# Strassen's held PSUM banks as tiles of their own, and narrow score tiles for the first twelve attention units

## The chip, the cores and the metric

The kernel runs on one core of one Trainium2 chip. The metric is the device time of one execution in microseconds. Time before: a median of 747.47 us over three runs (745.8 to 748.61).

## The reference

Window attention with eight heads (four with a plain window of 32 keys, four with every fourth key of the last 128), then a feed-forward layer that takes the maximum of three products. Everything is fp32.

```python
# q, k, v: [8, 8, 576, 64]
rel = pos[:, None] - pos[None, :]
mask_plain = (rel >= 0) & (rel < 32)                       # heads 0 to 3
mask_dil = (rel >= 0) & (rel < 128) & (rel % 4 == 0)       # heads 4 to 7
scores = where(mask, q @ k.T / 8, -1e9)
attn = softmax(scores) @ v
x = attn.transpose(0, 2, 1, 3).reshape(4608, 512)
h = maximum(maximum(x @ w1, x @ w2), x @ w3)               # w1, w2, w3: [512, 768]
out = h @ w_out                                            # w_out: [768, 512]
```

## The kernel before

**Number format.** An fp32 product is made of three matmuls on a high and a low part of each operand: high by high, high by low, low by high. All large matmuls therefore come in threes.

**Attention.** The work is cut in 64 units: half a batch (288 tokens) times a pair of heads, NPAIR = 4 pairs to a half. A unit takes scores into a couple of PSUM banks (one bank per head of the pair), reduces the maximum, takes exponentials, sums, normalises, turns the weights around (keys to partitions) and multiplies by the values; the result goes, split in high and low parts, into x. The first LEAN = 12 units are made by `dense` (L588): blocks of 96 queries by 128 keys (72 by 104 in the dilated heads), masks added by a matmul with the identity (L622), scores (L629), three passes of VectorE over 768 or 832 columns (L646, L465, L662), transposes on TensorE through a second couple (L711), a copy back, values (L735); forms C and D normalise afterwards, with sums from TensorE (L745). A letter of FORMS per unit picks the variant. The other units are made by `attention` and `behind` (L841, L888): tiles of 32 queries by 64 keys, 96 rows of three query blocks at a time, half as many columns, masks at L861, scores at L875, maximum L908, exponentials L919 or L931, and six 32x32 transposes on VectorE (L970) into PT, whose unused places stay zero; values at L982. They come in visits of two units (`visited`, `products`), whose matmuls stand together in TensorE's order.

**Feed-forward, plain part.** The first 1152 tokens (four halves) go through `ffn` (L1032) in three tiles of 384 tokens: up projections at L1048 in the two banks of the tag "ffn", then down at L1101.

**Feed-forward, Strassen part.** The other 3456 tokens go in four passes of 864. In each, nine blocks of the up projections (six feature pairs are three double rows times the three weights) are made with seven products instead of eight: `combine` (L1216) forms the token sums, `multiplied` (L1312) the products, each six matmuls of 128x432 (L1348). Products accumulate across each other in PSUM. D (product 0) and A (product 1) go to the two "ffn" banks; bB and bC are held for a whole pass:

```python
held = [buf("b", f"held{i}") for i in range(2)]
```

The order on TensorE is, per block: 0 into D, 1 into A, 6 of the block before into bC, 2 into bB, 3 into A, 4 into bC, 5 into bB. Between them ScalarE copies bB<-bA after product 1 (`ab`, L1430) and bC<-bB after product 2 (`bc`, L1437), both by the line L458. VectorE (L465) takes the maximum or the sum out of the banks: the put of product 6 reads bC after product 6 and has to come before `bc` overwrites it. After each pass the down projection runs (L1491). The product weights come from DRAM, 256 KB each, on the queue of SP into six slots, reused in turn.

**PSUM.** Eight banks: three tiles `banks_0` to `banks_2` of two banks each (couples, tag "b", six slots), and two `bank_i` of one (tag "ffn"). A request of width 2 takes a couple, one of width 1 half of one. Waits are set by tile: an instruction that touches one half of a couple is ordered behind earlier work on either half by another engine. bB and bC are the halves of one couple. Matmuls whose output is named "banks" write into couples.

**Order.** Nothing is issued as it is described: each step is handed to a planner (`Plan`, L112) with its cost by engine, its dependencies and its buffers. `deadlines` works due times back from the feed-forward steps, with a slack per kind of step (UNIT_SLACK, COMBINE_SLACK and so on); the planner then picks, step by step, the engine and the step that can start soonest, the most urgent first, chooses slots (`couple`, `single`), and issues in that order. Where TensorE would stand idle for long in the early part it adds a filler matmul (L1595), which keeps the array busy and computes nothing. The costs are estimates in the code: they set the order, and the chip's semaphores do the rest.

Of the kernel before, what the change touches and what calls it, by code (L numbers as in the profile page):

```python
# [34 lines left out]
SLOTS = 6  # L35
TAKEN = 70
# [4 lines left out]
FORMS = "adDaaaAaCADA"  # L41
# [7 lines left out]
SPILL = 0.103  # L49
# [3 lines left out]
UNIT_PACE, UNIT_SLACK, UNIT_LEAD = 1.728, 2.588, 2.639  # L53
FILL = 0.22
BURSTS, BURST = (21, 35), 16
WEIGHT_PACE, WEIGHT_SLACK, WEIGHT_LEAD = 0.544, 0.749, 1.374
# [7 lines left out]
class Buf:  # L64


    def __init__(self, pool, tag, limit, shape, dtype, name):
        self.pool, self.tag, self.limit = pool, tag, limit
        self.shape, self.dtype, self.name = shape, dtype, name
        self.users = 0  # L70
        self.number = None
        self.end = 0.0
        self.slot = None
        self.t = None
        self.width = 1

# [35 lines left out]
class Plan:  # L112
# [54 lines left out]
    def room(self, st, slots):  # L167
# [6 lines left out]
        for tag in set(new):  # L174
            k = new.count(tag)
            left = slots[tag]
            for b in st.bufs:
                if b.tag == tag and b.slot is None and b.width == 2:
                    t, i = self.couple(left)
# [6 lines left out]
    def couple(self, free):  # L186

        when = {i: t for t, i in free}
        return min(((max(t, when[i + 1]), i) for i, t in when.items() if not i % 2 and i + 1 in when), default=(1e9, 0))

    def single(self, free, at):

        held = {i for _, i in free}
        return min(free, key=lambda x: (max(x[0], at), x[1] ^ 1 in held, x))
# [30 lines left out]
    def order(self, fill=None):  # L225
# [11 lines left out]
        order = []  # L237
        live, since = {"dve": None, "pool": None}, 0.0
        fills, must, bursts = 0, 0, list(BURSTS)
        while len(order) - fills < len(self.steps):  # L240
            best = None
            for e, cands in waiting.items():
                now = free[e]
                for st in cands:
# [3 lines left out]
                    if st.bufs:  # L248
                        at = max(at, self.room(st, slots))
# [34 lines left out]
            for b in sorted(st.bufs, key=lambda b: -b.width):  # L284
                if b.slot is None:
                    if b.width == 2:
                        b.slot = self.couple(slots[b.tag])[1]
                    else:
                        b.slot = self.single(slots[b.tag], at)[1]
                    slots[b.tag] = [x for x in slots[b.tag] if not 0 <= x[1] - b.slot < b.width]  # L290
                    self.given[b.tag] = self.given.get(b.tag, 0) + 1
            if e == "sp":
# [30 lines left out]
            for b in st.bufs:  # L323
                b.users -= 1
# [20 lines left out]
def tile_dilated_window_attention__then__maxout_ffn(  # L345
# [78 lines left out]
    KEPT["b"] = [x[:, i] for x in couples for i in range(2)] + couples  # L424
# [29 lines left out]
    nc.gpsimd.memset(strips[:, 0, :WIN], NEG)  # L454

# [132 lines left out]
    def dense(u):  # L588

        half, p = divmod(u, NPAIR)  # L590
        b, hf = divmod(half, 2)
        dil = int(p >= 2)
        nb, nq, wk = (4, 72, 104) if dil else (3, 96, 128)
        nw = nb * wk
        k_step = 104 if dil else 96
        form = FORMS[u]
        runs = [(0, 2)] if form.islower() else [(0, 1), (1, 2)]
        blockwise, late = form in "bdBD", form in "cdCD"
        kb, kload, v, vload = loads(u, (None, None))
        W, mx, sm = buf("W", f"W{u}"), buf("mx", f"mx{u}"), buf("sm", f"sm{u}")  # L600
        sp, tp = (buf("b", f"{x}{u}", width=2) for x in ("s", "pt"))

        def S4(j0, j1):
            return sp.t[:96, j0:j1, :nw].rearrange("p j (n k) -> p j n k", k=wk)

        def W4(j0, j1):
            return W.t[:nq, nw * j0 : nw * j1].rearrange("p (j n k) -> p j n k", j=j1 - j0, k=wk)

        def by_row(x, j0, j1):
            return x.t[:nq, j0 * nb : j1 * nb].rearrange("p (j n) -> p j n", j=j1 - j0)  # L610

        def spread(x, j0, j1):
            return by_row(x, j0, j1).unsqueeze(3).broadcast_to([nq, j1 - j0, nb, wk])

        def scores(_):

            for j in range(2):
                if dil or hf:
                    m = masks[:96, hf : hf + 1, :wk].broadcast_to([96, nb, wk])
                else:  # L620
                    m = masks[:96, :nb, :wk]
                nc.tensor.matmul(  # L622
                    S4(j, j + 1)[:, 0], identb[:96, :96], m, start=True, stop=False, skip_group_check=True
                )
            for i in range(nb):
                for j in range(2):
                    d = slice(64 * j, 64 * j + 64)
                    k0 = HALF + k_step * i
                    nc.tensor.matmul(  # L629
                        S4(j, j + 1)[:nq, 0, i],  # L630
                        kb.t[d, nq * i : nq * i + nq],
                        kb.t[d, k0 : k0 + wk],
                        start=False,
                        stop=True,
                        skip_group_check=True,
                    )

        s = plan.add(
            {"pe": 0.3 + 2 * nw * 0.000435 + nb * (wk / 600 + 0.01)}, scores, [kload], [kb, mx, W, sp], rows=96
        )  # L640
        expd, last = [], []
        for j0, j1 in runs:
            n = nw * (j1 - j0)

            def most(_, j0=j0, j1=j1):
                nc.vector.tensor_reduce(  # L646
                    by_row(mx, j0, j1), S4(j0, j1)[:nq], axis=mybir.AxisListType.X, op=ALU.max, negate=True
                )

            def eighth(e, j0=j0, j1=j1):  # L650
                a = mx.t[:nq, j0 * nb : j1 * nb]
                (nc.vector if e == "dve" else nc.gpsimd).tensor_scalar(a, a, 0.125, None, ALU.mult)

            def less(_, j0=j0, j1=j1):
                tt("dve", W4(j0, j1), S4(j0, j1)[:nq], spread(mx, j0, j1), ALU.add)

            def expo(_, j0=j0, j1=j1):
                a = W.t[:nq, nw * j0 : nw * j1]
                nc.scalar.activation(a, a, AF.Exp, scale=0.125)

            def total(_, j0=j0, j1=j1):
                nc.vector.tensor_reduce(by_row(sm, j0, j1), W4(j0, j1), axis=mybir.AxisListType.X, op=ALU.add)  # L662

            t = plan.add({"dve": dve(n)}, most, [s], [sp, mx])
            if blockwise:
                t = plan.add({"dve": 0.165, "pool": 0.22}, eighth, [t], [mx])
                for m in range(j0 * nb, j1 * nb):

                    def expo_b(_, m=m):
                        j, i = divmod(m, nb)  # L670
                        nc.scalar.activation(
                            W.t[:nq, wk * m : wk * m + wk],
                            S4(j, j + 1)[:nq, 0, i],
                            AF.Exp,
                            bias=mx.t[:nq, m : m + 1],
                            scale=0.125,
                            accum_out=sm.t[:nq, m : m + 1],
                        )

# [976 lines left out]
```

## Time and profile before

| | |
|---|---|
| median of three runs | 747.47 us |
| the profiled execution | 746.38 us |
| its span | 744.6 us |
| granted TensorE clock, mean | 0.997 |
| TensorE matmuls busy | 706.9 us, 95% |
| VectorE busy | 506.9 us, 68% |
| GpSimd busy | 294.6 us, 40% |
| ScalarE busy | 291.3 us, 39% |
| first matmul of the plain feed-forward | at 54.04 us |
| moved by DMA | 140.30 MB, 188 GB/s |

PE is the matmul side of TensorE, PEld its weight loads, DVE is VectorE, ACT ScalarE, POOL GpSimd, SP the queue that issues the DMAs. In a timeline a row is a run of like instructions: start, length, how many, and in brackets how long the engine had been idle and what ended that. The length of a run of matmuls reaches a little past the start of the next run, since matmuls overlap; differences of starts are exact. In the chain of waits each row is a stretch of the path that ends last. A row of the waits reads: who waited for whom, microseconds in total, times, longest.

### The profile page before, as it was taken

Reading aid. Unit: us, or ns where it says so; the run is one execution under the profiler, and the core shown is the slowest. Engines: PE = TensorE matmul, PEld = TensorE weight load, DVE = VectorE, ACT = ScalarE, POOL = GpSimd, SP = SyncE. Lnnn points to the kernel's source line nnn. Section 1 sums busy time; section 2 is a strip of 40 time slices with the busy share of each in tenths; the row PEclk is TensorE's granted clock in tenths of the full one; section 3 lists DMA queues with packets and bytes.
Section 4 is the critical chain, followed back from the end, with each engine's and each line's share of the span. In section 5 each row is a group of like instructions: output and inputs, shape, how many; then the busy total and the mean of one; then the engine's idle time right before and its main releaser. Section 6 shows DMA issues by size and latency. Waiting matters only on the chain.

```text
span 744.6 us, 16812 instructions
## 1 busy us (share of the span) xinstructions
PE 706.9 (95%) x6492; PEld 602.3 (81%) x6492; DVE 506.9 (68%) x943; ACT 291.3 (39%) x1015; POOL 294.6 (40%) x376
## 2 busy tenths in 40 slices
PE   8979999999999999999999999899999989999998
PEld 5549888998998987887888888688888868888876
DVE  6978899879778665678766567996756795223240
ACT  5566643433345524335443434253343423122211
POOL 3778866674128111167510205761020475001042
PEclk9999999999999999999999999999999999999999
DMA  9969936536623778672487777248776613666511
GB/s 322 327 205 357 328 122 211 175 113 219 198 63 100 228 217 258 210 219 100 141 240 222 238 221 215 71 138 239 218 238 194 183 54 98 200 194 198 169 44 53
DMA packets 83807, 140.30 MB, mean 188 GB/s; under 512 B 7952, under 2 KB 32272, under 8 KB 83728
## 3 DMA queue, kind: packets, MB, share of 16 engines
q1 hardware_dynamic: 83728, 139.23, 60.0%
q8 instruction: 51, 0.84, 0.5%
q14 instruction: 28, 0.23, 0.1%
HBM read 113.25 MB, written 25.95 MB: 187 GB/s over the span
## 4 chain that ended last, share of the span: by engine, by line
PE 76%; DVE 10%; POOL 5%; ACT 4%; issue 2%; DMA 2%; SPq 0%; POOLq 0%; DVEq 0%; ACTq 0%
PE banks L1348 25%; PE bank L1348 14%; PE bank L1491 11%; PE bank L1048 10%; PE bank L1101 4%; PE banks L982 4%; ACT banks L458 3%; PE banks L875 3%; PE bank L1595 2%; DVE PT L970 2%; DVE h L465 2%; DVE hx L465 2%; DMA wS<-tmps 1%; POOL wu L465 1%; DVE tmps L465 1%
## 5 line engine op out<-in xcount | busy, mean ns | idle before, releaser
L1348 PE MATMUL banks<-t,wm 128*128 128x432 f32 x864 | 195.8, 368 | 20.3 <-ACT banks L458 14.5
L1348 PEld LDWEIGHTS banks<-t,wm 128*128 128x128 f32 x864 | 156.7, 188 | 49.9 <-ACT banks L458 33.6
L1348 PE MATMUL bank<-t,wm 128*128 128x432 f32 x648 | 139.9, 360 | 0.0
L970 DVE STREAM_TRANSPOSE PT<-W 32x192 f32<-32x192 f32 (+1 forms) x312 | 125.1, 401 | 7.2 <-POOL W L465 1.6
L1348 PEld LDWEIGHTS bank<-t,wm 128*128 128x128 f32 x648 | 121.5, 188 | 6.3
L1491 PE MATMUL bank<-wdn,h 128*128 128x512 f32 (+1 forms) x504 | 119.6, 394 | 4.9 <-DVE h L465 3.0
L1048 PE MATMUL bank<-xa,wu 128*128 128x384 f32 x648 | 118.2, 338 | 0.5 <-ACT tmps L458 0.5
L1491 PEld LDWEIGHTS bank<-wdn,h 128*128 128x128 f32 (+1 forms) x504 | 91.9, 184 | 29.6 <-DVE h L465 4.2
L1048 PEld LDWEIGHTS bank<-xa,wu 128*128 128x128 f32 x648 | 111.7, 188 | 2.8 <-ACT tmps L458 1.1
L931 ACT ACTIVATE W<-banks,mx 96x64 f32<-96x64 f32 x286 | 85.0, 315 | 30.4 <-PE banks L1348 12.1
L912 POOL TENSOR_SCALAR mx<-mx 96x8 f32<-96x8 f32 (+1 forms) x35 | 8.6, 245 | 139.6 <-DVE mx L908 139.5
L931 ACT ACTIVATION_READ_ACCUMULATOR W<-banks,mx 96x1 f32 x286 | 59.2, 207 | 0.0
L458 ACT COPY tmps<-bank 128x432 f32<-128x432 f32 (+1 forms) x51 | 25.8, 507 | 83.5 <-PE bank L1348 73.8
L465 POOL TENSOR_TENSOR W<-W,sm 96x384 f32<-96x384 f32 (+4 forms) x39 | 40.1, 1031 | 37.0 <-DVE sm L957 33.5
L908 DVE TENSOR_REDUCE mx<-banks 96x6 f32<-96x384 f32 (+1 forms) x52 | 30.0, 614 | 33.2 <-PE banks L875 33.2
L465 DVE TENSOR_TENSOR tmps<-banks,tmps 128x432 f32<-128x432 f32 (+1 forms) x52 | 30.6, 591 | 29.5 <-PE banks L1348 29.3
L460 POOL TENSOR_SCALAR h<-hx 128x256 fp32r<-128x256 f32 (+1 forms) x24 | 9.8, 415 | 94.0 <-DVE hx L465 88.3
L465 POOL TENSOR_TENSOR h<-hx,h 128x256 fp32r<-128x256 f32 (+1 forms) x52 | 40.9, 808 | 14.4 <-PE bank L1491 10.9
L952 POOL TENSOR_TENSOR sm<-sm,small_c 96x8 f32<-96x8 f32 (+1 forms) x46 | 12.1, 264 | 83.4 <-ACT W L931 68.1
L458 ACT COPY o<-bank 128x512 f32<-128x512 f32 (+1 forms) x35 | 20.5, 584 | 51.6 <-PE bank L1491 34.2
L465 DVE TENSOR_TENSOR hx<-banks,hx 128x432 f32<-128x432 f32 x24 | 14.5, 606 | 37.6 <-PE banks L1348 37.6
L1101 PE MATMUL bank<-wdn,h 128*128 128x512 f32 x162 | 38.6, 395 | 0.0
(137 smaller groups left out, 943.2 us busy)
## 6 DMA issues: line engine op xcount, KB each, us to landing
wm<-wS SPq DMA_DIRECT2D x252, 256.0 KB
k<-in_qk_d_dram SPq DMA_DIRECT2D x32, 352.0 KB
k<-in_qk_p_dram SPq DMA_DIRECT2D x32, 304.0 KB
wS<-tmps SPq DMA_DIRECT2D x18, 512.0 KB
st<-in_w_up_dram SPq DMA_DIRECT2D x14, 512.0 KB
v<-in_v_d_dram SPq DMA_DIRECT2D x32, 208.0 KB
out_dram<-o SPq DMA_DIRECT2D x25, 256.0 KB
v<-in_v_p_dram SPq DMA_DIRECT2D x32, 192.0 KB
```

The source lines that it names most:

```text
L458: nc.scalar.copy(dst, src)
L465: (nc.vector if eng == "dve" else nc.gpsimd).tensor_tensor(dst, a, b, op=op)
L875: nc.tensor.matmul(sp.t[32 * r : 32 * r + rows, j, at + 64 * n : at + 64 * n + nk], kb.t[d, q0 : q0 + rows], kb.t[d, k0 : k0 + nk], start= ...
L908: nc.vector.tensor_reduce(by_row(mx), S4(), axis=mybir.AxisListType.X, op=ALU.max, negate=True)
L931: nc.scalar.activation(W3()[:, m], S4()[:, m // nb, m % nb], AF.Exp, bias=mx.t[:96, m : m + 1], scale=0.125, accum_out=sm.t[:96, m : m + 1],)
L970: nc.vector.transpose(PT.t[c : c + 32, : 2 * nb, 32 * i : 32 * i + 32], W3()[32 * i : 32 * i + 32, :, 32 * e : 32 * e + 32],)
L982: nc.tensor.matmul(pv.t[64 * j : 64 * j + 64, nq * i : nq * i + nq], v.t[:wk, j, i, :], PT.t[:wk, nb * j + i, :nq], start=True, stop=True,)
L1048: nc.tensor.matmul(bank.t[:, :n], wu[f].t[:, g, wz, c, :], xa[c].t[:, xz, t0 : t0 + n], start=(m == 0 and c == 0), stop=(m == 2 and c == 3),)
L1101: nc.tensor.matmul(bank.t, hv(hs[f], hz)[:, s0 : s0 + 128], wdn[f].t[:, wz], start=(f == 0 and m == 0), stop=(f == NF - 1 and m == 2),)
L1348: nc.tensor.matmul(bank.t[:, :HP], wv[:, wz, c], t_of(i, xz)[:, c], start=(start and m == 0 and c == 0), stop=(m == 2 and c == 1), skip_gr ...
L1491: nc.tensor.matmul(bank.t[:rows], hz.t[:, f, :rows], wdn[f].t[:, wz], start=(f == 0 and m == 0), stop=(f == NF - 1 and m == 2),)
L1595: nc.tensor.matmul(idle.t, identb, masks.rearrange("p n k -> p (n k)"), start=True, stop=True)
```

## The change

1. **The held banks.** PSUM is now two couples and two tiles `single_0` and `single_1` of one bank. bB gets `single_0` and bC `single_1` as a fixed home, so neither shares a tile. Small outputs such as a unit's values may use the singles before the Strassen part begins.
2. **The planner** knows of the tile that a couple shares: `shared` and `seen_by` delay a step until the other engines have finished their last work on either half, and `single` prefers a bank that is free of this.
3. **The first twelve units** are made by `attention` and `behind`, one unit to a visit, and `dense` is gone. FORMS has a new meaning: a lower-case letter turns the weights with six 32x32 transposes on VectorE (u4, u5, u7 to u11), an upper-case one with transposes on TensorE through a couple and four copies (u0 to u3, u6). Four memsets on GpSimd clear the PT buffers at the start.
4. **Numbers of the planner**: slacks, paces and costs, among them 0.05 instead of 0.25 us for a visit's fixed cost and 12.5 instead of 14.0 ns for a small score matmul.

```diff
+COUPLES = 2
-FORMS = "adDaaaAaCADA"
+FORMS = "AAAAaaAaabaa"
-TILE_NS = 14.0
+TILE_NS = 12.5
-COMBINE_SLACK, PREPARE_SLACK, LOAD_SLACK = 25.759, 134.466, 0.15
+COMBINE_SLACK, PREPARE_SLACK, LOAD_SLACK = 12.814, 72.124, 0.5
...
-UNIT_PACE, UNIT_SLACK, UNIT_LEAD = 1.728, 2.588, 2.639
+UNIT_PACE, UNIT_SLACK, UNIT_LEAD = 2.0, 1.802, 5.094
...
+        for b in st.bufs:
+            if b.slot is None and b.home is not None:
+                at = max(at, next((t for t, i in slots[b.tag] if i == b.home), 1e9))
...
+    def shared(self, i, e):
+
+        return max((t + self.AFTER[o] + TO_PE * (e == "pe") for o, t in self.seen[i].items() if o != e), default=0.0)
...
-    couples = [ps.tile([128, 2, 512], F32, name=f"banks_{i}", bufs=1) for i in range(3)]
+    couples = [ps.tile([128, 2, 512], F32, name=f"banks_{i}", bufs=1) for i in range(COUPLES)]
...
+    singles = [ps.tile([128, 512], F32, name=f"single_{i}", bufs=1) for i in range(6 - 2 * COUPLES)]
+    KEPT["b"] = [x[:, i] for x in couples for i in range(2)] + singles + couples
...
+    for t in KEPT["PT0"][::-1] + KEPT["PT1"]:
+        nc.gpsimd.memset(t, 0.0)
...
+    def early(u):
+
+        sp = buf("b", f"s{u}", width=2)
+        first, rest, _ = attention(u, (None, None), sp, 0, 1)
+        s = plan.add({"pe": first[1] + 0.25}, lambda _: first[0](), *first[2:])
+        return rest(s)
...
+            tp = buf("b", f"tp{u}", width=2)
+
+            def transposes(_):
+                for m in range(2 * nb):
+                    c = 96 * (m % nb)
+                    nc.tensor.transpose(tp.t[:64, m // nb, c : c + 96], W3()[:, m], ident[:96, :96])
...
-                x_of[divmod(u, NPAIR)] = products([dense(u)])[1][0](())
+                x_of[divmod(u, NPAIR)] = products([early(u)])[1][0](())
...
     held = [buf("b", f"held{i}") for i in range(2)]
+    for i, x in enumerate(held):
+        x.home = 2 * COUPLES + i
```

**How it moves instructions.** Three places, first of before and then of the change. ScalarE, near the end of the third Strassen pass; `tmps`, `hx` and `raw` are buffers in SBUF, bank_103 and bank_104 (bank_104 and bank_105 in the change) the two "ffn" banks, and the brackets name the engines whose semaphores the copy waits for. Before:

```order
L458 COPY tmps_102<-bank_103 128x432 [waits PE_49]
L458 COPY banks_97<-bank_104 128x432 [waits DVE_49,PE_49]
L458 COPY banks_97<-banks_97 128x432 [waits DVE_49]
L458 COPY hx_3068<-bank_104 128x432 [waits PE_49]
L458 COPY raw<-banks_99 128x288 [waits PE_49]
```

After, the same copies:

```order
L490 COPY tmps_103<-bank_104 128x432 [waits PE_49]
L490 COPY single_99<-bank_105 128x432 [waits DVE_49,PE_49]
L490 COPY single_100<-single_99 128x432 [waits DVE_49,PE_49]
L490 COPY hx_3238<-bank_105 128x432 [waits PE_49]
L490 COPY tmps_102<-bank_104 128x432 [waits PE_49]
```

The sequence of copies is as it was. The second row is bB<-bA, the third bC<-bB; what were two halves of banks_97 are single_99 (bB) and single_100 (bC), and bC<-bB now waits for VectorE and TensorE apart, where one semaphore of VectorE stood for both.

TensorE at the start of the program, without fillers and weight loads; k0 to k3, W and v belong to the units u0 to u3, the digit in banks_0_97 is the couple. Before:

```order
L622 MATMUL banks_0_97<-masks_68,identb_67 96x384
L629 MATMUL banks_0_97<-k0_118 96x128 x6
L622 MATMUL banks_1_98<-masks_68,identb_67 96x384
L629 MATMUL banks_1_98<-k1_120 96x128 x6
L622 MATMUL banks_2_99<-masks_68,identb_67 96x416
L629 MATMUL banks_2_99<-k2_122 72x104 x8
L711 MATMUL banks_1_98<-ident_66,W_1_90 128x96 x6
L711 MATMUL banks_0_97<-ident_66,W_0_89 128x96 x6
L735 MATMUL banks_0_97<-PT0_0_93,v0_147 64x96 x6
```

After:

```order
L696 MATMUL banks_0_97<-strips_69,identb_67 32x192
L710 MATMUL banks_0_97<-k0_123 32x64 x18
L696 MATMUL banks_1_98<-strips_69,identb_67 32x192
L710 MATMUL banks_1_98<-k1_125 32x64 x18
L710 MATMUL banks_0_97<-k2_127 32x64 x4
L710 MATMUL banks_1_98<-k3_129 32x64 x4
L818 MATMUL banks_0_97<-ident_66,W_0_89 64x96 x6
L818 MATMUL banks_1_98<-ident_66,W_1_90 64x96 x6
L838 MATMUL banks_0_97<-PT0_0_93,v0_168 64x96 x6
```

Scores of u0 to u3 still stand ahead of the first transposes; they go through two couples instead of three, and the masks are rows of 32.

TensorE around the first matmul of the plain feed-forward (L1048 before, L904 in the change), again without fillers and weight loads; the number behind k and v is the unit. Before:

```order
L622 MATMUL banks_2_99<-masks_68,identb_67 96x384
L629 MATMUL banks_2_99<-k9_357 96x128 x6
L735 MATMUL banks_0_97<-PT1_1_96,v7_584 64x72 x8
L1048 MATMUL bank_0_103<-xa0_296,wu0_320 128x384
L622 MATMUL banks_0_97<-masks_68,identb_67 96x416
L629 MATMUL banks_0_97<-k10_422 72x104 x8
L711 MATMUL banks_2_99<-ident_66,W_3_92 128x96 x6
```

After:

```order
L710 MATMUL banks_1_98<-k9_488 32x64 x18
L838 MATMUL single_1_100<-PT1_0_95,v6_660 64x72 x8
L838 MATMUL single_0_99<-PT1_1_96,v7_683 64x72 x8
L696 MATMUL banks_0_97<-strips_69,identb_67 32x256
L710 MATMUL banks_0_97<-k10_590 32x64 x4
L904 MATMUL bank_0_104<-xa0_362,wu0_351 128x384
L838 MATMUL single_1_100<-PT0_0_93,v8_709 64x96 x6
L710 MATMUL banks_0_97<-k11_644 32x64 x4
```

The scores of u10 have moved ahead of the feed-forward's first matmul, u11's still follow it, and no transposes of TensorE follow it any more. Over the whole program the change has 121 fillers for 96 and 354 transposes on VectorE for 312.

More of the change, by code (lines that the diff above doesn't have):

```diff
@@ L75, in __init__ @@
         self.width = 1
+        self.home = None
     def take(self):
@@ L178, in room @@
                 if b.tag == tag and b.slot is None and b.width == 2:
-                    t, i = self.couple(left)
+                    t, i = self.couple(tag, left)
                     left = [x for x in left if not 0 <= x[1] - i < 2]
@@ L183, in room, with couple, single, key @@
                 at = max(at, sorted(left)[k - 1][0] if len(left) >= k else 1e9)
-        return at
-    def couple(self, free):
-        when = {i: t for t, i in free}
+        for b in st.bufs:
+            if b.slot is None and b.home is not None:
+                at = max(at, next((t for t, i in slots[b.tag] if i == b.home), 1e9))
+        return at
+    def couple(self, tag, free):
+        when = {i: t for t, i in free if tag != "b" or i < 2 * COUPLES}
         return min(((max(t, when[i + 1]), i) for i, t in when.items() if not i % 2 and i + 1 in when), default=(1e9, 0))
-    def single(self, free, at):
+    def single(self, tag, free, at, e):
         held = {i for _, i in free}
-        return min(free, key=lambda x: (max(x[0], at), x[1] ^ 1 in held, x))
+        def key(x):
+            t = max(x[0], at)
+            if tag == "b" and x[1] < 2 * COUPLES:
+                return (max(t, self.shared(x[1] // 2, e)), x[1] ^ 1 in held, x)
+            return (t, tag == "tmp" and x[1] ^ 1 in held, x)
+        return min(free, key=key)
+    def shared(self, i, e):
+        return max((t + self.AFTER[o] + TO_PE * (e == "pe") for o, t in self.seen[i].items() if o != e), default=0.0)
+    def seen_by(self, st, e, at):
+        for b in st.bufs:
+            if b.tag == "b" and b.slot is not None and b.slot < 2 * COUPLES:
+                at = max(at, self.shared(b.slot // 2, e))
+        return at
     def after(self, e, o, n, end):
@@ L237, in order @@
         order = []
+        self.seen = [{} for _ in range(COUPLES)]
         live, since = {"dve": None, "pool": None}, 0.0
@@ L248, in order @@
                     if st.bufs:
-                        at = max(at, self.room(st, slots))
+                        at = self.seen_by(st, e, max(at, self.room(st, slots)))
                     if best is not None and (at, st.due) >= best[:2]:
@@ L285, in order @@
                 if b.slot is None:
-                    if b.width == 2:
-                        b.slot = self.couple(slots[b.tag])[1]
+                    if b.home is not None:
+                        b.slot = b.home
+                    elif b.width == 2:
+                        b.slot = self.couple(b.tag, slots[b.tag])[1]
                     else:
-                        b.slot = self.single(slots[b.tag], at)[1]
+                        b.slot = self.single(b.tag, slots[b.tag], at, e)[1]
                     slots[b.tag] = [x for x in slots[b.tag] if not 0 <= x[1] - b.slot < b.width]
                     self.given[b.tag] = self.given.get(b.tag, 0) + 1
+            at = self.seen_by(st, e, at)
             if e == "sp":
@@ L323, in order @@
             for b in st.bufs:
+                if b.tag == "b" and b.slot < 2 * COUPLES:
+                    self.seen[b.slot // 2][e] = max(end, self.seen[b.slot // 2].get(e, 0.0))
                 b.users -= 1
@@ L892, in behind @@
         nw = 128 * nb
-        form = LATER[(u - LEAN) % len(LATER)]
+        form = FORMS[u] if u < LEAN else LATER[(u - LEAN) % len(LATER)]
         def S4():
@@ L924, in behind @@
         t = plan.add({"dve": dve(nw)}, most, [s], [sp, mx])
-        if form == "b":
+        if form in "bB":
             t = plan.add({"pool": 0.22, "dve": 0.165}, eighth, [t], [mx])
@@ L1000, in products @@
         s = plan.add(
-            {"pe": sum(x[1] for x in parts) + 0.25},
+            {"pe": sum(x[1] for x in parts) + 0.05},
             run,
```

207 lines of the change are left out of this document (24 added, 183 removed).

## The prediction

> **What bounds the kernel now.** I began with the share of busy time by engine in six stretches of the span, because an average over this program hides its stages. The columns are the stretch, its length, then busy time (and instructions) of PE, PEld, DVE, ACT and POOL, the granted clock, the share of the DMA engines and GB/s.
>
> ```profile
> 0.00:54.00 54.00, 47.98 (x448) 28.54 (x448) 43.10 (x69) 30.52 (x74) 33.15 (x50) 0.97 0.82 283
> ...
> 239.00:340.00 101.00, 95.71 (x999) 83.79 (x996) 68.00 (x144) 42.09 (x174) 27.26 (x42) 1.00 0.74 222
> ...
> 367.00:484.00 117.00, 109.97 (x1157) 94.76 (x1156) 79.81 (x160) 44.15 (x179) 33.47 (x53) 1.00 0.66 199
> ...
> 497.00:613.00 116.00, 109.04 (x1076) 93.52 (x1077) 81.55 (x162) 43.38 (x178) 33.21 (x53) 1.00 0.63 188
> ...
> 626.00:712.00 86.00, 80.17 (x385) 70.82 (x384) 25.34 (x45) 18.72 (x38) 4.37 (x7) 1.00 0.61 177
> ```
>
> The first row is the start, up to the first matmul of the plain FFN. The other four are the product stages of the four Strassen passes; in the first three attention is woven in, in the last there is none. There TensorE is busy 94 to 95% of the time, the other engines far less, DVE at most 70%. What TensorE does not do in these four stretches is 5.29 + 7.03 + 6.96 + 5.83 = 25.1 us. The last one is telling: DVE and ACT have under a third of the work there, and TensorE idles as much. So it is not load, it is something that the product loop does to itself. The groups and the waits say what:
>
> ```profile
> L1348 PE MATMUL banks<-t,wm 128*128 128x432 f32 x864 | 195.8, 368 | 20.3 <-ACT banks L458 14.5
> ...
> L1348 PE MATMUL bank<-t,wm 128*128 128x432 f32 x648 | 139.9, 360 | 0.0
> ```
>
> ```profile
> ACT banks L458 <- PE banks L1348: 47.4, 28, 2.9
> ACT banks L458 <- DVE hx L465: 44.2, 20, 3.8
> ...
> PEld banks L1348 <- ACT banks L458: 33.6, 49, 1.0
> ```
>
> The same matmul of the same shape has idle time in front of it where it writes into a couple ("banks"), and none where it writes into a bank of its own ("bank"). TensorE waits for ScalarE's copies between the held banks (49 times), and these copies wait for TensorE and for VectorE. The chain of waits in the last pass shows how (start, length, what):
>
> ```profile
> 647.21 1.46 PE banks L1348 x6
> ...
> 652.58 2.37 PE bank L1348 x12
> 654.95 1.20 PE banks L1348 x6
> 656.16 0.51 ACT banks L458
> 656.72 1.46 PE banks L1348 x6
> ...
> 658.21 0.62 DVE hx L465
> ...
> 658.85 0.51 ACT banks L458
> 659.40 2.63 PE banks L1348 x12
> ...
> 694.50 1.45 PE banks L1348 x6
> ```
>
> At 652.58 products 0 and 1 run in their own banks. Product 1 has ended by 654.95 and the copy bB<-bA needs nothing but that, yet it starts at 656.16, when product 6 has ended, which writes bC, the other half of the same couple. Product 2 waits for the copy. Then the put of product 6 (a VectorE max out of bC) could run from 656.2, but starts at 658.21, when product 2 in bB has ended; the copy bC<-bB comes at 658.85, and products 4 and 5 wait for it until 659.40. Both pauses come from one tile that holds both banks.
>
> **The change, part by part.** *Held banks as two tiles.* One product is six matmuls; 12 in 2.37 us make 0.1975 us each, so a block's 42 take 8.30 us. From 647.21 to 694.50 lie five blocks, 9.46 us each: 1.16 us are lost per block, 10.4 us over the pass's nine. An attended block:
>
> ```profile
> 390.57 1.45 PE banks L1348 x6
> ...
> 393.19 1.15 PE banks L982 x32
> 394.34 0.28 PE banks L861 x6
> 394.62 0.79 PE banks L875 x68
> 395.42 2.56 PE banks L1348 x12
> ...
> 402.12 1.46 PE banks L1348 x6
> ```
>
> It takes 11.55 us; the visit of two attention units in it (393.19 to 395.42) is 2.23, so 11.55 - 2.23 - 8.30 = 1.02 is lost. The idle time of the three attended stretches is 19.28 us, 0.71 for each of 27 blocks; the recorded ends of a run of matmuls reach about 0.27 into the pause (1.46 for six that issue in 1.18), so 0.71 is low. I take 0.9, an estimate between the two: 24.3 us. Together 35 us of stalls, with bounds of 25 (the recorded idle time) and 38 (27 x 1.02 + 10.4).
>
> What is late next, when the copies wait for their own bank alone? The copy bB<-bA can run beside product 6: 1.20 of cover against the 0.56 from 656.16 to 656.72, 0.64 to spare. The put from bC can run beside product 2. The copy bC<-bB comes after product 2 and hides under product 3, 1.18 against 0.55 plus the 0.28 by which the drained end (658.18) trails the last issue: 0.35 to spare. In the last pass nothing else stands in ACT's way. In the attended ones an exponential or another copy may, and 0.35 is little: I leave one block in four 0.5 us, 36 x 0.25 x 0.5 = 4.5. So 35 - 4 = 31 us go. The price of the edit elsewhere: attention had the other two couples beside the held one and has two still, so nothing is lost in the passes. The loads of product weights come in every 8.4 instead of 9.46 us: 177 GB/s become some 199 in the last pass, and 222 some 244 in the first (101 us to 92). The first row above has 283, so nothing is charged.
>
> *The first twelve units.* Their prices, in one timeline around the first FFN matmul (start, length, what; later starts give the true lengths):
>
> ```profile
> 54.04 1.07 PE L1048 MATMUL bank<-xa,wu 128*128 128x384 f32 x4
> 55.75 0.51 PE L622 MATMUL banks<-masks,identb 96*96 96x416 bf16 x2 [0.65 <-DVE xa L465]
> 56.19 0.94 PE L629 MATMUL banks<-k 64*72 64x104 f32 x16
> 57.06 3.22 PE L1048 MATMUL bank<-xa,wu 128*128 128x384 f32 x17
> ...
> 61.33 0.66 PE L711 MATMUL banks<-ident,W 96*128 96x96 f32 x6
> 61.78 5.13 PE L1048 MATMUL bank<-xa,wu 128*128 128x384 f32 x28
> ...
> 77.31 0.72 PE L735 MATMUL banks<-PT,v 128*64 128x96 f32 x12
> 77.85 0.67 PE L745 MATMUL banks<-ident,sm 96*64 96x96 f32 x12
> 78.45 0.99 PE L1048 MATMUL bank<-xa,wu 128*128 128x384 f32 x4
> ```
>
> ```profile
> 40.00:60.00 20.00, 17.03 (x155) 11.41 (x156) 17.40 (x29) 13.69 (x27) 16.23 (x17) 0.91 0.77 247
> ```
>
> A dense unit costs TensorE 1.31 us of scores (55.75 to 57.06), 0.45 of transposes, 0.54 of values, and 0.60 of sums where its form has them. By the attended block above, two units of the new form cost 1.07 for scores and 1.15 for values: 0.54 and 0.58 each, and none or 0.45 for transposes. After 54.04 TensorE has no slack left, so what counts is what stays behind that point: now the scores of u10 and u11 (2.6), four sets of transposes (1.8), of values (2.2) and two of sums (1.2), 7.8 us. In the new order u11's scores and four sets of values stay, 0.54 + 4 x 0.58 = 2.9, since u8 to u11 are turned on VectorE. That is 5 us less.
>
> Does the first FFN matmul still come at 54? TensorE has slack ahead of it (fillers). VectorE:
>
> ```profile
> L646 DVE TENSOR_REDUCE mx<-banks 96x6 f32<-96x768 f32 x4 | 3.7, 945 | 4.4 <-PE banks L629 4.4
> ```
>
> ```profile
> L970 DVE STREAM_TRANSPOSE PT<-W 32x192 f32<-32x192 f32 (+1 forms) x312 | 125.1, 401 | 7.2 <-POOL W L465 1.6
> ...
> L908 DVE TENSOR_REDUCE mx<-banks 96x6 f32<-96x384 f32 (+1 forms) x52 | 30.0, 614 | 33.2 <-PE banks L875 33.2
> ```
>
> A dense unit passes three times over 768 columns, 2.8 us; a new one three times over half as many, 1.84, and seven of twelve add six transposes, 2.4. Net 7 x 1.45 - 5 x 0.96 = +5.4 us, some of it after the FFN's start, against 10.9 us of idle VectorE in the first 54 us. The four memsets lie on GpSimd, idle 20.9 of 54 us. The 25 more fillers stand where TensorE has nothing else to do. I take the start as unmoved, from -3 to +5. A pause at the start also slows TensorE: 20 us at 0.91 are 3.6 us at half the clock, so one more such stretch would cost up to 1.8. The Trainium skill, "TensorE: Matmul & The Clock Gate", Part 1, has this as a rule: one idle window of about 3.4 us halves the clock; this row agrees, and with one gap of that length more the result would by the rule be 713.3 instead of 711.5.
>
> **Sum.** The profiled execution took 746.38, with 744.6 of span and 1.8 around it; the median is 747.47, 1.1 above. 746.4 - 31 (stalls) - 5 (early units) = 710.4, plus 1.1: **711.5 us**. The planner's other new constants move due times, and I give them nothing.
>
> **The rivals.**
> *New waits take half of it back (0.18).* The copies and puts stand in one program order with the attention's steps on ScalarE and VectorE. The rows of the attended passes show VectorE 67 to 70% busy, and it would do the same work in less time, some 76%; a put or copy that stands behind one 0.4 us transpose or one exponential too many has lost its 0.35. If half of the 35 us stays: 746.4 - 17.5 - 3 + 1.1 = 727, between 720 and 735. For it: VectorE's load. Against it: the 0.64 of the other copy, and the last pass, where nothing is queued. The Trainium skill, the same page, "Architectural detail", says that ScalarE and VectorE queues are strict and that TensorE alone pulls weight loads ahead; it speaks for this rival, but no row quoted here shows a copy held up that way, so it adds nothing to the 0.18.
> *Slower: two couples starve the first units (0.03).* Scores take a couple, and so do the transposes of five units (u0 to u3, u6). If units then go one at a time, each with its chain of reductions, exponentials and turning, the 48 us from 6 to 54 would near double: 746.4 + 48 - 31 + 1.1 = 764. It decides from an FFN start later than 54 + 31 + 5 + 4 = 94. Against it: the new order issues the scores of u2 and u3 ahead of the transposes of u0 and u1.
> *The wait stays (0.05).* If the pauses came from something other than the shared tile, the early units alone are left: 746.4 - 5 + 1.1 = 742.5. Against it: the idle time of 0.0 of the same matmuls in banks of their own, and the split wait in the new order of ScalarE.
>
> **How the numbers follow.** The forecast has 0.74: its own range goes from 746.4 - 38 - 9 + 1.1 = 700 (every stall gone, early gain with a start 3 to 4 us sooner) to 746.4 - 25 + 0 + 1.1 = 722.5 (the lower bound, nothing early). To leave out no more than 2 in 10 I reach into the first rival to 727, and down to 699. Left out are the upper half of that rival (0.09), the two others (0.08) and little below. A measurement can tell 0.5%, 3.7 us, from no change. Forecast and first rival are faster by more; of the third about half (0.02 to 0.03) falls inside 3.7: faster 0.94, same 0.03, slower 0.03.
>
> **What would show it.** In the changed profile the product matmuls of 128x432 should have the same idle time, near none, in every kind of tile; the wait of PEld for ACT's copies should fall from 33.6 to under 10 us; the last pass should repeat at 8.3 to 8.6 us per block instead of 9.46; the copy bB<-bA should start as product 1 ends, beside product 6. The first FFN matmul should start at 51 to 59 us, with under 4 us of unit work on TensorE after it. A block time of 9 us or more in the last pass makes the mechanism wrong; 8.4 there with over 0.5 lost in attended blocks makes the first rival right; a start beyond 60 us makes my reading of the early units wrong.

## The result

The changed kernel takes 701.19 us (median of four runs, 700.8 to 701.51), the kernel before 747.29 beside it: a ratio of 0.938, 95% interval 0.9365 to 0.9402. That is 46.1 us less. The time lies 10.3 us below the forecast of 711.5 and inside the range of 699 to 727. The profiled execution took 701.34 us with 699.6 of span.

From the page of the changed kernel, the engines and the groups of its product matmuls (busy, mean ns; idle before them and its main releaser):

```profile
PE 683.6 (98%) x6797; PEld 599.4 (86%) x6797; DVE 502.7 (72%) x983; ACT 287.8 (41%) x990; POOL 277.9 (40%) x354
...
L1204 PE MATMUL single<-t,wm 128*128 128x432 f32 x864 | 183.4, 360 | 0.6 <-DVE single L494 0.6
...
L1204 PE MATMUL bank<-t,wm 128*128 128x432 f32 x648 | 140.6, 360 | 0.8 <-DVE t L497 0.8
L1347 PE MATMUL bank<-wdn,h 128*128 128x512 f32 (+1 forms) x504 | 119.9, 394 | 1.9 <-POOL h L497 1.9
```

Ahead of the product matmuls into the held banks 20.3 us of idle time have become 0.6, and with those into the other banks it is 1.4 in all. The wait of PEld for ScalarE's copies, 33.6 us before, is gone from the list of waits. Of the copies into the held tiles the waits now read:

```profile
ACT single L490 <- PE single L1204: 33.2, 27, 1.9
...
ACT single L490 <- PE bank L1204: 26.2, 36, 2.0
```

The 36 copies bB<-bA all wait for a "bank", which is where product 1 writes, and no longer for product 6. The stretches that answer to those of before, each from the pass's first product to about its first down projection, with the start of the program ahead of them (columns as before):

```profile
0.00:50.78 50.78, 45.81 (x792) 25.41 (x792) 41.99 (x87) 29.85 (x64) 35.69 (x57) 1.00 0.97 338
232.75:318.00 85.25, 83.87 (x846) 77.74 (x845) 65.36 (x139) 38.22 (x149) 19.43 (x30) 1.00 0.79 240
354.15:437.00 82.85, 82.85 (x843) 77.47 (x842) 61.84 (x136) 38.74 (x150) 15.76 (x29) 1.00 0.81 244
473.44:556.00 82.56, 82.56 (x842) 77.18 (x841) 61.56 (x135) 38.75 (x150) 15.49 (x29) 1.00 0.79 239
591.63:667.00 75.37, 75.37 (x383) 71.83 (x382) 29.74 (x50) 18.46 (x37) 6.19 (x8) 1.00 0.68 202
```

In the last three rows the record has TensorE busy all the time. The chain of waits in the last pass consists of TensorE alone:

```profile
604.78 2.37 PE single L1204 x12
607.15 2.36 PE bank L1204 x12
609.50 2.37 PE single L1204 x12
611.87 1.18 PE bank L1204 x6
613.05 2.37 PE single L1204 x12
...
646.14 2.37 PE single L1204 x12
```

Five blocks from 604.78 to 646.14 make 8.27 us each, against 9.46. The timeline of one block shows where the copies went:

```profile
609.34 2.53 PE L1204 MATMUL single<-t,wm 128*128 128x432 f32 x12
609.54 0.50 ACT L490 COPY single<-bank 128x432 f32<-128x432 f32 x1 [0.61 <-PE bank L1204]
610.80 0.61 DVE L497 TENSOR_TENSOR hx<-single,hx 128x432 f32<-128x432 f32 x1 [2.22 <-PE single L1204]
611.71 1.34 PE L1204 MATMUL bank<-t,wm 128*128 128x432 f32 x6
611.91 0.50 ACT L490 COPY single<-single 128x432 f32<-128x432 f32 x1 [1.86 <-PE single L1204]
612.89 2.53 PE L1204 MATMUL single<-t,wm 128*128 128x432 f32 x12
```

The run of twelve at 609.34 is products 6 and 2. The copy bB<-bA runs at 609.54 under product 6, the put of product 6 at 610.80 under product 2, the copy bC<-bB at 611.91 under product 3, and ends 0.48 us before product 4 starts.

### The profile page after: what moved, and what is told of

It reads as the page before. It is cut to its first block, busy times and chain, and to the rows that moved or that the text cites. A ratio compares the mean times of both kernels' runs of the same rounds, so it can differ in the third digit from the quotient of the medians.

```text
span 699.6 us, 17412 instructions
## 1 busy us (share of the span) xinstructions
PE 683.6 (98%) x6797; PEld 599.4 (86%) x6797; DVE 502.7 (72%) x983; ACT 287.8 (41%) x990; POOL 277.9 (40%) x354
## 4 chain that ended last, share of the span: by engine, by line
PE 82%; DVE 9%; POOL 4%; DMA 2%; issue 2%; ACT 0%; POOLq 0%; ACTq 0%; DVEq 0%
PE single L1204 24%; PE bank L1204 18%; PE bank L1347 17%; PE bank L904 11%; PE banks L710 3%; PE banks L838 3%; PE bank L957 3%; DVE tmps L497 3%; DVE PT L806 2%; DMA wS<-tmps 1%; PE single L838 1%; PE banks L696 1%; POOL wu L497 1%; DVE W L497 1%; PE bank L1453 1%
## 5 line engine op out<-in xcount | busy, mean ns | idle before, releaser
L1204 PE MATMUL single<-t,wm 128*128 128x432 f32 x864 | 183.4, 360 | 0.6 <-DVE single L494 0.6
L1204 PEld LDWEIGHTS single<-t,wm 128*128 128x128 f32 x864 | 161.8, 188 | 9.8 <-DVE single L494 1.0
L806 DVE STREAM_TRANSPOSE PT<-W 32x192 f32<-32x192 f32 (+1 forms) x354 | 141.6, 400 | 7.9 <-POOL W L497 2.0
L904 PE MATMUL bank<-xa,wu 128*128 128x384 f32 x648 | 117.4, 338 | 2.4 <-DVE tmps L497 2.4
L904 PEld LDWEIGHTS bank<-xa,wu 128*128 128x128 f32 x648 | 111.9, 188 | 5.3 <-DVE tmps L497 3.9
L766 ACT ACTIVATE W<-banks,mx 96x64 f32<-96x64 f32 x292 | 86.5, 311 | 9.5 <-PE bank L1204 6.1
L743 DVE TENSOR_REDUCE mx<-banks 96x6 f32<-96x384 f32 (+1 forms) x64 | 37.3, 614 | 58.2 <-PE banks L710 58.1
L497 POOL TENSOR_TENSOR h<-hx,h 128x256 fp32r<-128x256 f32 (+1 forms) x53 | 42.4, 823 | 14.2 <-PE bank L1347 13.7
L787 POOL TENSOR_TENSOR sm<-sm,small_c 96x8 f32<-96x8 f32 (+1 forms) x44 | 10.8, 245 | 91.8 <-ACT W L766 77.6
L492 POOL TENSOR_SCALAR h<-hx 128x256 fp32r<-128x256 f32 (+1 forms) x29 | 13.3, 474 | 83.3 <-DVE hx L497 72.3
L497 POOL TENSOR_TENSOR W<-W,sm 96x512 f32<-96x512 f32 (+1 forms) x33 | 33.8, 1024 | 16.0 <-DVE sm L792 14.7
L957 PEld LDWEIGHTS bank<-wdn,h 128*128 128x128 f32 x162 | 30.0, 188 | 8.5 <-DVE h L497 1.6
L710 PE MATMUL banks<-k 64*32 64x64 f32 (+1 forms) x2688 | 35.2, 217 | 0.0
```

The lines of the kernel that those rows point to most:

```text
L492: nc.gpsimd.tensor_scalar(dst, src, 1.0, 1.0, ALU.mult, ALU.mult)
L497: (nc.vector if eng == "dve" else nc.gpsimd).tensor_tensor(dst, a, b, op=op)
L710: nc.tensor.matmul(sp.t[32 * r : 32 * r + rows, j, at + 64 * n : at + 64 * n + nk], kb.t[d, q0 : q0 + rows], kb.t[d, k0 : k0 + nk], start= ...
L743: nc.vector.tensor_reduce(by_row(mx), S4(), axis=mybir.AxisListType.X, op=ALU.max, negate=True)
L766: nc.scalar.activation(W3()[:, m], S4()[:, m // nb, m % nb], AF.Exp, bias=mx.t[:96, m : m + 1], scale=0.125, accum_out=sm.t[:96, m : m + 1],)
L806: nc.vector.transpose(PT.t[c : c + 32, : 2 * nb, 32 * i : 32 * i + 32], W3()[32 * i : 32 * i + 32, :, 32 * e : 32 * e + 32],)
```

## The experiments

Each kernel ran against the kernel before on the same chip (746.7 us in each of these experiments; the first row is from the measurement beside the change). The last three columns cut each profiled execution at the starts of the first matmul of the plain feed-forward, of the first product and of the last product of the Strassen part. The last stretch, called the passes below, has the product loops of the four passes and the three down projections between them; the down projection that follows the last product takes 29 us before and after.

| kernel | median us | first feed-forward matmul at | from there to the first product | first to last product |
|---|---|---|---|---|
| before | 747.29 | 54.0 | 185.1 | 472.5 |
| the change | 701.19 | 50.8 | 182.0 | 433.8 |
| change, held banks in one tile | 741.55 | 52.9 | 182.0 | 470.8 |
| before, held banks split alone | 727.90 | 64.9 | 183.7 | 443.9 |
| change, all old numbers | 712.35 | 54.8 | 189.7 | 432.4 |
| change, three couples | 758.30 | 54.7 | 193.8 | 476.6 |
| change, planner without the new rule | 720.03 | 53.9 | 185.9 | 447.5 |
| change, all twelve upper case | 703.38 | 50.7 | 181.5 | 435.5 |
| change, all twelve lower case | 709.79 | 53.6 | 189.0 | 431.9 |
| change, old unit numbers | 703.21 | 54.0 | 180.6 | 434.4 |
| change, old costs | 710.85 | 56.5 | 187.3 | 432.3 |
| change, eight upper case | 702.24 | 48.9 | 185.4 | 433.0 |
| change, seven upper case | 705.86 | 45.7 | 192.6 | 432.6 |
| change, dense units and old numbers | 740.07 | 81.2 | 181.7 | 442.0 |

My theory was that the one tile of bB and bC makes the pauses; the main rival that the retuned order removes them.

**The held banks in one tile again.** The planner's order of instructions stays as it is in the change.

```diff
-    singles = [ps.tile([128, 512], F32, name=f"single_{i}", bufs=1) for i in range(6 - 2 * COUPLES)]
+    pair = ps.tile([128, 2, 512], F32, name="single_0", bufs=1)
+    singles = [pair[:, i] for i in range(2)]
```

> The changed kernel with one edit: the two held banks are again the two halves of one tile; the issue order on every engine stays that of the changed kernel. Theory (the shared tile makes the pauses in the product loop): all that the passes gained goes back, the last pass repeats at 9.4 to 9.5 us per block, idle time ahead of the product matmuls near 20 us again, 735 to 741 us. Rival (the retuned order removed the pauses): the order is unchanged here, so the time stays within 5 us of 701.

Measured 741.55 us, ratio to before 0.9935 (0.9919 to 0.9952). The pauses are back; the groups of this kernel and its chain:

```profile
L1205 PE MATMUL single<-t,wm 128*128 128x432 f32 x864 | 193.9, 367 | 22.0 <-ACT single L491 18.9
...
L1205 PE MATMUL bank<-t,wm 128*128 128x432 f32 x648 | 140.7, 360 | 1.1 <-DVE t L498 1.1
```

```profile
641.40 1.46 PE single L1205 x6
...
642.95 0.62 DVE hx L498
...
643.59 0.51 ACT single L491
...
644.15 2.62 PE single L1205 x12
...
650.91 1.46 PE single L1205 x6
```

A block takes 9.51 us (641.40 to 650.91), with the put and the copy on the path as before. The passes lose 37.0 us, and the feed-forward starts 2.2 us later. The order alone does not remove the pauses: the rival falls, and with all else of the change in place the tile is worth 40 of the 46 us.

**The split alone, in the kernel before.** Two couples, two singles, the homes; nothing else.

```diff
-    couples = [ps.tile([128, 2, 512], F32, name=f"banks_{i}", bufs=1) for i in range(3)]
+    couples = [ps.tile([128, 2, 512], F32, name=f"banks_{i}", bufs=1) for i in range(2)]
+    singles = [ps.tile([128, 512], F32, name=f"single_{i}", bufs=1) for i in range(2)]
...
     held = [buf("b", f"held{i}") for i in range(2)]
+    for i, x in enumerate(held):
+        x.home = 4 + i
```

> The kernel before with two couples and two single banks as the homes of bB and bC, and nothing else of the change (dense first units and old numbers kept). Theory: the passes gain 33 to 39 us as in the changed kernel, 8.3 us per block in the last pass; the dense units then have two couples for scores and transposes, and the planner puts 156 fillers for 96, 60 at some 0.25 us, so the first feed-forward matmul comes 8 to 15 us later: 717 to 724 us. Rival (the retuned planner is needed for the passes too): blocks lose 0.5 us or more, 730 us or above.

Measured 727.9 us (ratio 0.9746, 0.9731 to 0.9761), 4 above the expected band and below the rival's. The start moved to 64.9 as expected; the passes gained 28.6, not 33 to 39. From its page:

```profile
L1355 PE MATMUL single<-t,wm 128*128 128x432 f32 x864 | 185.5, 361 | 1.3 <-ACT single L465 1.3
...
L1355 PE MATMUL bank<-t,wm 128*128 128x432 f32 x648 | 140.1, 360 | 1.7 <-DMA wm<-wS 1.7
...
L1498 PE MATMUL bank<-wdn,h 128*128 128x512 f32 (+1 forms) x504 | 120.0, 395 | 6.9 <-DVE h L472 4.5
```

The pauses of the product loop are all but gone here too (3.0 us of idle time), and the last pass repeats at 8.27 us per block. But ahead of the down projections TensorE idles 6.9 us, against 1.9 in the change; the kernel without the rule, below, shows the same wait. The later start is the price of the third couple: dense units with two couples begin the feed-forward 10.9 us later.

**All the old numbers, and two parts of them.** The cut of the diff shows the unit numbers and the costs, which also ran alone; the run with all of them puts the other slacks and paces back too.

```diff
-TILE_NS = 12.5
+TILE_NS = 14.0
-UNIT_PACE, UNIT_SLACK, UNIT_LEAD = 2.0, 1.802, 5.094
+UNIT_PACE, UNIT_SLACK, UNIT_LEAD = 1.728, 2.588, 2.639
...
-            {"pe": sum(x[1] for x in parts) + 0.05},
+            {"pe": sum(x[1] for x in parts) + 0.25},
```

> The changed kernel with all the planner's numbers of before (slacks, paces, cost of small matmuls, visit costs), with its tiles, its early units and its new rules kept. Theory: the product loop stays free of pauses; what the numbers bought is the shorter wait ahead of the down projections (4 us) and a part of the earlier feed-forward start (141 fillers for 121): 705 to 711 us. Rival (the numbers carry the gain in the passes): 715 us or above, with over 0.4 us lost per block.

> The changed kernel with only the pace, slack and lead of the attention units as before. Theory (they set how early the first units' steps are due against the weights' steps, and so the start of the feed-forward): the first feed-forward matmul comes 3 to 5 us later, the stretch from there to the first product is 2 to 6 us longer, the passes stay: 705 to 711 us. Rival (the cost numbers of small matmuls and visits carry the early gain): within 2 us of 701.

> The changed kernel with the planner's costs of small matmuls and of a visit as before (14.0 ns, 0.12 and 0.25 us), all else as changed. Theory (the too high costs make the planner expect TensorE late and put the units' matmuls and fillers, 142 for 121, accordingly): most of the 11 us that all old numbers cost together, since the old unit numbers alone cost 2: 706 to 712 us, all of it before the first product. Rival (no single set of numbers carries it): within 3 us of 701.

All old numbers: 712.35 us (0.954, 0.952 to 0.956), a little over the band. But the split was not as expected: the passes are 1.4 us shorter than in the change, down projections included, and all 11.7 us are lost ahead of the first product. In this kernel the numbers therefore do nothing for the passes. The old unit numbers alone: 703.21 (0.9415, 0.9396 to 0.9435), start 3.2 later and the stretch behind it 1.4 shorter; my theory expected 705 to 711. The old costs alone: 710.85 (0.9526, 0.9497 to 0.9555), 9.7 us, as expected, start 5.7 and stretch 5.3 longer. 2.0 and 9.7 add up to 11.7, close to the 11.2 of all. That costs nearer to the truth give a better order is argued, not shown: only their effect is, and about half of it comes by long pauses (below).

**Three couples, held banks in one of them.**

```diff
-COUPLES = 2
+COUPLES = 3
-    for i, x in enumerate(held):
-        x.home = 2 * COUPLES + i
```

> The changed kernel with three couples and without homes, so that bB and bC share a couple, and the planner plans for that. Theory: the early units and the new numbers are all that is left, 736 to 744 us, with 9.2 to 9.5 us per block in the last pass. Rival (a planner that knows of the shared tile can place the copies so that they hide): 9.0 us per block or less, 725 us or below.

758.3 us, 1.5% slower than before (1.0152, 1.0128 to 1.0175), worse than either theory. The passes lose all that they had gained and 4 us more (476.6 us). This planner knows of the shared tile and does not hide its copies. The rest is in the plain feed-forward, 193.8 us, where TensorE pauses for 6.1 and 3.9 us; the run with seven upper-case units below shows the same kind of pause.

**The planner without the new rule.**

```diff
-        return max((t + self.AFTER[o] + TO_PE * (e == "pe") for o, t in self.seen[i].items() if o != e), default=0.0)
+        return 0.0
```

> The changed kernel with a planner that knows nothing of the tile that a couple shares (its delay for that is 0); tiles, homes, early units and numbers kept. Theory (this rule, not the numbers, spares the waits ahead of the down projections and of the last few products): the passes lose 5 to 9 us of what they gained, the first feed-forward matmul comes 0 to 4 us later for 10 fillers more: 706 to 714 us. Rival (the rule is bookkeeping only): 699 to 704 us, and the early units or the homes are what the passes have ahead of the split alone.

720.03 us (0.9645, 0.9621 to 0.9668): 18.8 lost, twice what I expected. The profiled execution, which took 722.02, loses 13.7 in the passes and 7.0 ahead of them. The stretch of the second pass from its first down projection to the next pass's products, first in this kernel, then in the one before, then in the change:

```profile
453.02:490.17 37.15, 33.72 (x243) 25.97 (x242) 33.13 (x48) 14.31 (x51) 28.25 (x29) 1.00 0.34 110
```

```profile
461.37:497.06 35.69, 33.60 (x243) 26.04 (x242) 32.41 (x44) 14.85 (x52) 28.62 (x29) 1.00 0.36 113
```

```profile
437.47:473.44 35.97, 35.49 (x370) 28.26 (x368) 26.46 (x44) 13.87 (x51) 21.98 (x26) 1.00 0.40 122
```

In the first two VectorE is busy 89 and 91% of the time, TensorE idles 3.4 and 2.1 us, and 110 small matmuls of attention are in it. In the change VectorE has 26.5 of 36 us, and TensorE does 236 of them with 0.5 us idle. The timeline of the kernel without the rule shows what a down projection waits for there:

```profile
468.84 3.13 DVE L806 STREAM_TRANSPOSE PT<-W 32x256 f32<-32x256 f32 x7
...
472.01 0.82 DVE L497 TENSOR_TENSOR h<-hx,h 128x256 fp32r<-128x256 f32 x2
...
472.88 0.50 PE L1347 MATMUL bank<-wdn,h 128*128 128x512 f32 x1 [1.04 <-DVE h L497]
```

The low part of h stands on VectorE behind seven transposes of an attention unit, and TensorE waits for it. So here what the planner believes of waits decides which work lands in which stretch.

**Which engine turns the first units.** One letter per unit: all twelve upper or lower case, the first eight upper, the first seven upper.

```diff
-FORMS = "AAAAaaAaabaa"
+FORMS = "AAAAAAAAABAA"
+FORMS = "aaaaaaaaabaa"
+FORMS = "AAAAAAAAabaa"
+FORMS = "AAAAAAAaabaa"
```

> The changed kernel with all twelve first units turned on TensorE through a couple (upper-case forms). Theory (VectorE sets when the first feed-forward matmul comes): 42 transposes of 0.4 us leave VectorE, the start comes 1 to 5 us earlier, and 4 x 0.45 us of transposes are added behind it on TensorE: 697 to 702 us. Rival (two couples starve units that take two each): start later than 55 us, 705 us or above.

> The changed kernel with all twelve first units turned on VectorE (lower-case forms). Theory (VectorE sets the start): 5 x 2.4 = 12 us are added to VectorE, 20 to 24 copies and 36 transposes leave ScalarE and TensorE, the planner puts 43 fillers more: the first feed-forward matmul comes 8 to 12 us later, 708 to 714 us. Rival (VectorE has slack enough there): within 3 us of 701.

> The changed kernel with the first eight units turned on TensorE and the last four on VectorE. Theory (VectorE's transposes ahead of the feed-forward are spared as in the run with all twelve on TensorE, and no transposes of TensorE are added behind its start): start at 49 to 51 us, 698 to 701 us, faster than the changed kernel by 0 to 3. Rival (the start is set by the loads from memory, whose share was 0.97 there): same start, 701 to 703 us.

> The changed kernel with u0 to u6 turned on TensorE and u7 to u11 on VectorE. Theory and rival as for the run with eight: 698 to 701 us if VectorE sets the start, 701 to 703 us if the loads do.

All upper: 703.38 (0.9421, 0.9394 to 0.9447); the start does not move, so neither side was right. All lower: 709.79 (0.950, 0.9479 to 0.9522) in the band, but the start is only 2.9 later; the other 7.0 lie behind it. Eight upper: 702.24 (0.9401, 0.9385 to 0.9416), start 1.8 earlier, no gain. Seven upper: 705.86 (0.9463, 0.944 to 0.9486), start 5.0 us earlier, and 4.7 us slower. So the number of VectorE's early transposes does not set the start, since with none of them it stays at 50.7; and the loads allowed one at 45.7. In the last kernel two pauses of TensorE, 6.4 and 3.4 us, eat the earlier start; the chain of waits at the first:

```profile
138.36 2.07 POOL tmps L492
...
140.51 2.35 POOL tmps L497
...
142.88 3.57 DMA wS<-tmps
...
146.68 0.49 ACT tmps L490
...
147.21 4.22 PE bank L904 x12
```

GpSimd makes a product weight of the Strassen part in a buffer `tmps`, a DMA stores it, ScalarE's copy out of a feed-forward bank needs that buffer, and TensorE needs the bank. No run of mine took this wait away.

Such pauses separate the rows of the table. In each of the seven kernels that need 185.4 us or more from the first feed-forward matmul to the first product, TensorE has one or two pauses of 2.3 to 6.4 us there, and with each the granted clock is half for 3.41 or 6.83 us. Eight of the ten wait for ScalarE's copy into `tmps`, two for VectorE's work on h. The change and the others that need 180.6 to 183.7 us have no pause longer than 2.01 there, and before (185.1) none above 0.82. With seven upper-case letters this accounts for the loss: 5.7 us more idle time than in the change and half of 10.2 us at half clock make 10.8, and the stretch is 10.6 longer. Eight upper-case letters have one such pause, of 5.15 us. Neither kernel with an earlier start is free of them, so what an earlier start alone is worth stays open, and so does what in the order brings a pause about.

**The split and the rule, with the dense units and the old numbers.** `dense` and its FORMS are put back into the kernel with the old numbers.

> The changed kernel with the dense first units of before put back and the old numbers: the held banks' own tiles and the planner's new rules alone. Theory: the passes take as long as in the run with the old numbers (188 us from first to last product), 7 us less than with the split alone; the dense units with two couples start the feed-forward 15 to 20 us later than in that run (190 fillers for 139): 722 to 730 us. So the early units are what pays for the third couple. Rival (the early units matter little): 710 to 716 us.

740.07 us (0.9918, 0.9893 to 0.9943), 10 beyond the band. The feed-forward starts at 81.2, and the passes take 442.0, not 432. The product loops are as short as with the old numbers (330.4 us from first to last product of each, added up, against 330.7); the rest lies in the stretches between them, where TensorE idles 9.9 of 111.6 us. The rule without the early units does not spare these waits, and why is open. Against the run with the old numbers, which differs in the first units alone, the early units are worth 27.7 us.

## Why the prediction was right, and where the sum was off

*The pauses come from one tile.* Right in every step: the cause, the two copies and the put, and what covers each afterwards. The run with one tile shows the cause with the order held fixed.

*The size of the stalls.* I took off 31 us; the passes gained 38.7. (One reading was off: in the last pass TensorE was busy 93% of the time, not 94 to 95%; the idle times are right.) Counted from start to start, the product matmuls with the idle time ahead of them take 335.6 us before and 301.3 after. That is 34.3, so the 35 us of stalls, with 0.9 for an attended block, was a good estimate. Two things were off. I left 4.5 us for blocks in which a copy would come late; the idle time of 0.6 and 0.8 us says that hardly one does. And 4.4 us of the gain lie elsewhere: attention's matmuls in the product loops and the stretches between the loops, together, take 133.6 us before and 129.7 after, since TensorE waits less ahead of the down projections. My sum has no term for that. Without the new rule they take 142.0, with the split alone 137.2, so it is the planner's doing and not that of the tiles. With one tile and the same order 36.4 of the 37.0 us lost lie in the product matmuls. The rival of new waits fell in the product loop, although VectorE is 75% busy there (61.84 of 82.85 us); the slack of `bc`, measured in the last pass, is 0.48 us.

*The early units.* I forecast 5 us less behind an unmoved start. The first product came 6.4 us earlier: the start 3.3 (at 50.8, just ahead of the 51 to 59 that I gave), the stretch behind it 3.1. That the total came near was luck, for it is the sum of larger terms that I did not see. With the old numbers the first product comes 5.3 us later than before (244.5 against 239.1); the numbers, to which I gave nothing, are worth 11.7 there, in large part by the pauses that their order avoids. This was the wrong step: "The planner's other new constants move due times, and I give them nothing." The new rule, which I did not price at all, is worth 18.8 us in this kernel, part of it again a pause of 5.3 us in the plain feed-forward.

*Two couples starve the first units.* As a forecast of the change this rival was wrong, the start came earlier. As a mechanism it is real: with dense units the start moves to 64.9, and to 81.2 with the rule. The early units are what makes the two single banks affordable (start at 54.8 with them, at 81.2 with the dense ones, both with the old numbers and the rule); that all twelve may turn through a second couple with the start still at 50.7 says that a couple is not scarce for them. That dense units hold a couple longer is argued, from three passes over 768 columns, and was not measured.

*The clock.* The mean granted clock of the start rose from 0.97 to 1.00, so the stretch at half clock that I allowed for did not come. Before, TensorE had one long pause ahead of the feed-forward:

```profile
41.58 0.72 PE L735 MATMUL banks<-PT,v 128*64 128x96 f32 x12 [2.35 <-ACT banks L529]
```

From 43.50 to 46.91 us the granted clock was 0.50. In the change no pause between the first matmul and the first of the feed-forward is as long as 0.9 us. The Trainium skill, "TensorE: Matmul & The Clock Gate", Part 1, ties half rate to an idle window of about 3.4 us. The trace has the half rate, for 3.41 us, but the pause ahead of it was 2.35 us: the row that I took as agreement does not bear out the length of the pause.

*The median.* I added the 1.1 us by which the profiled execution of before lay under the median; the median after is 0.15 below the profiled one, which is 1.2 of the difference of 10.3. The passes are 7.7 of it, the early part 1.4.

## What to carry to other kernels

Two accumulators that are read and written in turn belong in tiles of their own where, as here, the wait is kept by tile: a neighbour's matmul holds up a copy that needs nothing of it. Look for a matmul of one shape that idles in one kind of tile and not in another. Where a planner orders the program, its beliefs about waits and costs are part of the change and want a price of their own; and moving one milestone forward is worth only what the next one follows: the seven upper-case units start the feed-forward 5.0 us earlier and end 4.7 us later, by two pauses on the way.

## What the runs showed of the hardware

TensorE can run such a mix without a recorded pause: 82.85 us busy of 82.85, with 843 matmuls for products, scores, masks and values, while VectorE was busy for 61.84 us and ScalarE for 38.74, in part with copies and sums out of neighbouring banks. Product matmuls into a tile of one bank take 360 ns of recorded time in the mean, as those into banks of their own did before, and 0.197 us from start to start (2.37 for twelve). All DMA traffic together ran at 239 to 244 GB/s in the attended stretches, 188 to 222 before, and at 202 in the last, 177 before. In the change no wait for a load of weights is among those of the product matmuls; with the split alone there is one, of 1.70 us.

The half clock came behind a pause of TensorE of 1.96 us in one run (eight upper-case letters, 42.91 to 44.87; granted clock 0.50 from 45.40 to 48.81), while a pause of 2.01 us (held banks in one tile, from 59.83) left it at 1.00. So in these runs the length of a pause alone does not decide it.
